# One redundant wait taken out of VectorE's program in a decode-block kernel

## The chip, the cores and the metric

The kernel runs on one core of one Trainium2 chip. The metric is the device time of one execution in microseconds; medians and ranges over several runs are given. VectorE is DVE in the profile, TensorE is PE (PEld for its weight loads), ScalarE is ACT, GpSimd is POOL, SyncE is SP. A letter q behind an engine's name means its sequencer.

## The reference, cut to what matters

One token (x, 640 wide) passes an attention block with a key and value cache and then a gated feed-forward block, each behind a layer norm:

```
h  = x + A(layernorm(x), k_cache, v_cache, wq, wo)   # 32 heads, 4096 cached positions, 128 wide
h2 = h + B(layernorm(h), w_gate, w_up, w_down)       # 640 -> 1728 -> 640
```

The caches and the weights are 84 MB, each byte used once. Only the first layer norm, that of x, has to do with the change.

## The kernel before: the parts concerned

The kernel records operations with their dependencies and emits waits for them. An operation whose function is `None` is a wait and nothing else.

```python
def _run(self, e, eng, ops, seen):
    for x in ops:
        ...
        for sem, c in self._need(eng, deps, seen).values():
            e.wait_ge(sem, c)
            seen[sem.name] = c
        if fn is None:
            continue
        inst = fn(e)
        if ev.used:
            inst.then_inc(ev.sem, 16 if ev.dma else 1)
```

GpSimd zeroes the tile `xlnB` first, then sets constants. TensorE spreads x over the partitions (`x_cols`), VectorE copies that out of PSUM, squares it, and so on to the normalised x, which is written into parts of `xlnB`:

```python
c_xz = GP(lambda e: e.memset(xlnB[:, :, :], 0.0))
c_one = GP(lambda e: e.memset(one_bf[:, :], 1.0))
...
xt = T(x_cols, d_x, c_one)
xc = V(lambda e: e.tensor_copy(xx[:, 0:5], ps_s[:, 0:5]), xt)

def layernorm(src, ev, out_fn, between=lambda: None):
    s2 = V(lambda e: e.tensor_mul(src[:, 5:10], src[:, 0:5], src[:, 0:5]), ev)      # "the square"
    m = T(lambda e: e.matmul(ps_s[:, 16:26], mean_f[:, :], src[:, 0:10], start=True, stop=True), s2, c_mean)
    ...                                                                             # 2 on VectorE, 2 on ScalarE
    return V(out_fn, l4)

xz = P.op("vector", None, c_xz)
xl = layernorm(xx, xc, lambda e: e.tensor_scalar(xlnB[...], xx[...], ln[:, 0:1], ln[:, 4:5], ALU.subtract, ALU.mult))
...
qd = T(q_proj, xl, d_wq)                       # the query projection, reads xlnB and wq
qa = VR(lambda e: e.tensor_copy(qb[...], ps_q), qd)
load_v(0, qd)                                  # first value load: into the place of wq
```

The softmax here doesn't subtract the row's maximum and nothing guards it: scores larger than these inputs give would overflow.

Of the kernel before, what the change touches and what calls it, by code (L numbers as in the profile page):

```python
# [180 lines left out]
def bass_sequential_preLN__gqa_block_cached__glu_gated_geglu__decode_kernel(nc, A_x, A_k_cache, A_v_cache, A_wq, A_wo, B_x, B_w_gate, B_w_up, B_w_down, out):  # L181
# [59 lines left out]
    P = Prog(nc)  # L241
# [31 lines left out]
    c_xz = GP(lambda e: e.memset(xlnB[:, :, :], 0.0))  # L273
# [56 lines left out]
    def layernorm(src, ev, out_fn, between=lambda: None):  # L330
        s2 = V(lambda e: e.tensor_mul(src[:, 5:10], src[:, 0:5], src[:, 0:5]), ev)
        m = T(lambda e: e.matmul(ps_s[:, 16:26], mean_f[:, :], src[:, 0:10], start=True, stop=True), s2, c_mean)
        l1 = V(lambda e: e.reduce_sum(ln[:, 0:2], ps_s[:, 16:26].rearrange("p (a c) -> p a c", a=2), axis=AX.X), m)
        l2 = V(lambda e: e.scalar_tensor_tensor(out=ln[:, 2:3], in0=ln[:, 0:1], scalar=ln[:, 0:1],
                                                in1=ln[:, 1:2], op0=ALU.mult, op1=ALU.subtract), l1)
        l3 = A(lambda e: e.activation(ln[:, 3:4], ln[:, 2:3], ACTF.Ln, bias=eps_t[:, 0:1], scale=-1.0), l2, c_eps)
        l4 = A(lambda e: e.activation(ln[:, 4:5], ln[:, 3:4], ACTF.Exp, bias=zero_t[:, 0:1], scale=-0.5), l3)
        between()
        return V(out_fn, l4)

    xz = P.op("vector", None, c_xz)
    xl = layernorm(xx, xc, lambda e: e.tensor_scalar(
        xlnB[:, :, :].rearrange("p c (a b) -> p c a b", a=4)[:, :, 0:4:3, :],
        xx[:, 0:5].unsqueeze(2).unsqueeze(3).to_broadcast([128, 5, 2, 16]), ln[:, 0:1], ln[:, 4:5],
# [257 lines left out]
```

## Time and profile before

| | before |
|---|---|
| time, median of 6 runs | 202.12 us (202.02 to 202.57) |
| span of the profiled run | 200.9 us |
| input queue's share of the DMA engines | 97.7% |
| VectorE busy | 103.6 us (52%) |
| wait records on VectorE's sequencer | 6 |
| copy of x to square of x, start to start | 0.28 us |

The lines behind the table stand in the prediction below. In the chain that ended last (the work followed back from the last instruction, each step to what released it), a row has a start, a length and what filled it; "issue" is time in which an engine waited for nothing that the profile shows. Rows of that chain near the end of the kernel before (VectorE's sequencer is DVEq), which the prediction did not look at, matter later:

```profile
196.33 0.03 issue
196.36 0.02 DVEq L114
196.38 0.04 issue
196.42 0.18 DVE hm L545
```

The second gate group ends on TensorE at 196.31 us (193.55 + 2.76 by the timeline), VectorE's sequencer serves a wait of 0.02 us, and 0.04 us later `hm` starts.

```profile
198.42 0.23 PEld L552 LDWEIGHTS psum<-k_all,hm 128*1 128x1 bf16 x12 [0.38 <-DMA k_all<-in_B_w_down_dram]
```

Here the down projection, started by `hm`, had to wait 0.38 us for a piece of its weights. So `hm` had a little time to spare in this execution, by this row up to 0.38 us as an estimate.

### The profile page before, as it was taken

What the parts mean: (1) busy time and instruction counts of PE and PEld (TensorE: products, weight loads), DVE (VectorE), ACT (ScalarE), POOL (GpSimd) and SP (SyncE); (2) the same over time, 40 slices, a digit from 0 to 9 for tenths busy, and PEclk for the clock granted to TensorE, in tenths of its full rate; (3) what the DMA queues carried; (4) which work ended last, traced back from release to release, by engine and by line L of the source; (5) the groups of instructions that cost most, each with busy time, mean ns of one, the idle gap of its engine ahead of it and who ended that gap; (6) DMA issues with size and microseconds to landing.
All of it is one profiled execution on the core that took longest, in us unless ns stands there. A gap on an engine that the chain in (4) does not pass through costs nothing.

```text
span 200.9 us, 2115 instructions
## 1 busy us (share of the span) xinstructions
PE 135.1 (67%) x1118; PEld 29.8 (15%) x742; DVE 103.6 (52%) x58; ACT 9.4 (5%) x27; POOL 7.4 (4%) x32
## 2 busy tenths in 40 slices
PE   0108001889897228997974588987899787787675
PEld 0103000000003100000022000000400000377573
DVE  0200001999942029799430599967798967020320
ACT  2100000000000100000001000000100000100100
POOL 6500000000000000000000000000000002000000
PEclk9999999999999855899999599999999999965555
DMA  9999999999999999999999999899999999999992
GB/s 351 424 478 418 418 418 418 418 431 496 483 447 418 418 431 418 418 418 418 431 418 418 483 483 444 346 424 424 418 516 418 418 418 401 416 436 417 427 404 98
DMA packets 2699, 84.31 MB, mean 420 GB/s; under 512 B 323, under 2 KB 518, under 8 KB 902
## 3 DMA queue, kind: packets, MB, share of 16 engines
q1 hardware_dynamic: 2690, 84.23, 97.7%
q8 instruction: 4, 0.07, 0.1%
q14 instruction: 1, 0.01, 0.0%
q10 hardware_dynamic: 4, 0.00, 0.0%
HBM read 84.23 MB, written 0.00 MB: 419 GB/s over the span
## 4 chain that ended last, share of the span: by engine, by line
DMA 65%; DVE 23%; PE 11%; issue 0%; ACT 0%; SPq 0%; DVEq 0%
DMA k_all<-in_A_k_cache_dram 42%; DVE prod L405 20%; DMA v_all<-in_A_v_cache_dram 13%; DMA v_all<-in_B_w_up_dram 9%; PE psum L167 4%; PE psum L389 4%; PE psum L531 1%; PE psum L552 1%; DVE sc L417 1%; DVE p_bd L424 1%; DVE sc L414 1%; DVE sc L415 1%; PE psum L371 0%; SPq L59 0%; ACT pt L418 0%
## 5 line engine op out<-in xcount | busy, mean ns | idle before, releaser
L405 DVE TENSOR_TENSOR prod<-k_all,qb 128x8192 bf16<-128x8192 bf16 x16 | 70.2, 4420 | 40.0 <-DMA k_all<-in_A_k_cache_dram 38.9
L167 PE MATMUL psum<-prod,id_b 128*128 128x512 bf16 x240 | 55.9, 387 | 0.0
L167 PE MATMUL psum<-none_b 128*128 128x512 bf16 x132 | 34.9, 419 | 0.0
L378 PE MATMUL psum<-none_b 128*128 128x512 bf16 x4 | 2.2, 549 | 26.1 <-DMA k_all<-in_A_k_cache_dram 26.1
L389 PE MATMUL psum<-v_all,p_bd 128*32 128x512 bf16 x256 | 14.5, 380 | 5.4 <-DVE p_bd L424 3.6
L417 DVE TENSOR_REDUCE sc<-psum 128x128 f32<-128x2048 f32 x6 | 13.7, 2286 | 5.2 <-PE psum L167 5.2
L371 PE MATMUL psum<-prod,id_b 128*128 128x512 bf16 x16 | 6.4, 400 | 9.5 <-DVE prod L405 6.7
L371 PEld LDWEIGHTS psum<-prod,id_b 128*128 128x128 bf16 x16 | 1.5, 96 | 75.5 <-DVE prod L405 47.9
L389 PEld LDWEIGHTS psum<-v_all,p_bd 128*32 128x32 bf16 x256 | 6.7, 97 | 37.5 <-DVE p_bd L424 31.6
L424 DVE TENSOR_TENSOR p_bd<-pt,own 128x1024 bf16<-128x1024 bf16 x8 | 9.8, 1221 | 2.2 <-ACT pt L418 2.2
L418 ACT ACTIVATE pt<-sc,zero_t 128x128 bf16<-128x128 f32 x8 | 3.2, 401 | 138.8 <-DVE sc L417 119.0
L354 PE MATMUL psum<-v_all,xlnB 128*32 128x512 bf16 x40 | 4.5, 630 | 6.7 <-DMA v_all<-in_A_wq_dram 6.7
L501 PE MATMUL psum<-aP,k_all 128*128 128x1 bf16 x160 | 6.7, 178 | 1.3 <-DMA k_all<-in_A_wo_dram 1.3
L460 POOL TENSOR_TENSOR RT<-RS,own 128x64 f32<-128x64 f32 x1 | 1.3, 1324 | 161.0 <-ACT pt L418 161.0
L501 PEld LDWEIGHTS psum<-aP,k_all 128*128 128x128 bf16 x160 | 6.6, 131 | 1.4 <-DMA k_all<-in_A_wo_dram 1.4
L395 PE MATMUL psum<-hs,po_sb 128*128 128x8 f32 x32 | 4.2, 258 | 3.2 <-ACT po_sb L458 3.2
L531 PE MATMUL psum<-hlnT,v_all 128*128 128x1 bf16 x150 | 5.5, 173 | 1.2 <-DMA v_all<-in_B_w_up_dram 1.2
L363 DVE CAST qb<-psum 128x512 bf16<-128x512 f32 x1 | 0.7, 690 | 9.7 <-PE psum L354 9.7
L531 PEld LDWEIGHTS psum<-hlnT,v_all 128*128 128x128 bf16 x150 | 5.4, 120 | 1.8 <-DMA v_all<-in_B_w_up_dram 1.3
L325 PE MATMUL psum<-one_bf,x_row 1*128 1x1 bf16 x5 | 0.4, 177 | 7.1 <-POOL own_g L308 7.1
L414 DVE TENSOR_REDUCE sc<-psum 128x64 f32<-128x1024 f32 x2 | 2.4, 1224 | 5.2 <-PE psum L167 5.2
L395 PEld LDWEIGHTS psum<-hs,po_sb 128*128 128x128 f32 x32 | 3.9, 191 | 5.1 <-issue 5.1
(75 smaller groups left out, 34.1 us busy)
## 6 DMA issues: line engine op xcount, KB each, us to landing
k_all<-in_A_k_cache_dram SPq DMA_DIRECT2D x2, 4096.0 KB, 20.6
v_all<-in_A_wq_dram SPq DMA_DIRECT2D x1, 5120.0 KB, 15.1
k_all<-in_A_wo_dram SPq DMA_DIRECT2D x2, 2560.0 KB, 29.2
v_all<-in_B_w_gate_dram SPq DMA_DIRECT2D x1, 2160.0 KB, 13.5
v_all<-in_B_w_up_dram SPq DMA_DIRECT2D x1, 2160.0 KB, 18.3
k_all<-in_B_w_down_dram SPq DMA_DIRECT2D x1, 800.0 KB, 21.0
k_all<-in_B_w_down_dram SPq DMA_DIRECT2D x1, 640.0 KB, 19.5
k_all<-in_B_w_down_dram SPq DMA_DIRECT2D x1, 480.0 KB, 21.7
```

The lines of the kernel that those rows point to most:

```text
L167: built = e.matmul(out, lhsT, rhs, start=start, stop=stop)
L354: i = e.matmul(ps_q[32 * t:32 * t + 32, :], xlnB[:, c, 32 * a:32 * a + 32], wq_j[:, c, t, a, :, :], start=(c == 0 and a == 0), stop=(c == ...
L371: mm = held if n or not first else lambda e, *a, **k: e.matmul(*a, **k)
L389: i = e.matmul(ps_o[a:a + 32, :], p_bd[:, s, 4 * b:4 * b + 4, :].rearrange("p g j -> p (g j)"), vt[:, 4 * b:4 * b + 4, :], start=(s == 0 a ...
L395: i = e.matmul(ps_a[:, bass.ds(at, 8)], po_sb[:, 128 * r:128 * r + 128], hs[:, r, :], start=(r == 0), stop=(r == 3))
L405: mults[j, s, i] = VM(lambda e: e.tensor_tensor(out=prod[:, i, :, :], in0=kt[:, 64 * c:64 * c + 64, :], in1=qb[:, j, :].unsqueeze(1).to_br ...
L414: V(lambda e: e.reduce_sum(sc[:, 64:128], g16(0, 1024), axis=AX.X), folds[j, s, 1], free)
L417: reds[j, s] = VR(lambda e: e.reduce_sum(sc[:, :], g16(0, 2048), axis=AX.X), folds[j, s, 1], free)
L418: exps[j, s] = AS(lambda e: e.activation(pt[:, :], sc[:, :], ACTF.Exp, bias=zero_t[:, 0:1], scale=INV_SQRT_DH, accum_out=RS[:, 2 * j + s:2 ...
L424: blocks[j, s] = VB(lambda e: e.tensor_tensor(out=p_bd[:, hf, :, :], in0=pt[:, :].unsqueeze(2).to_broadcast([128, 128, 8]), in1=own8[:, :] ...
L501: r = e.matmul(ps_p[:, c:c + 1], wo_sb[:, i, c::5], aP[:, i:i + 1], start=False, stop=(i == 31), skip_group_check=True)
L531: i = e.matmul(ps[:, m:m + 1], ws, hlnT[:, c:c + 1], start=(c == 0 and m == 0), stop=(c == 4), skip_group_check=True)
```

## The change

The tile is zeroed on GpSimd before `one_bf` is set: in the trace of the kernel before the two end at 1.64 and 1.66 us. TensorE's `x_cols` waits for `one_bf` (it starts at 7.09 us) and VectorE's copy waits for `x_cols` (7.48 us), so what stands behind the copy ran behind the zeroing too. By these times the wait is redundant; that the two always end in this order was not shown beyond the traces. The change takes the wait out to make VectorE's program one instruction shorter.

```diff
@@ -338,7 +338,6 @@
         between()
         return V(out_fn, l4)
 
-    xz = P.op("vector", None, c_xz)
     xl = layernorm(xx, xc, lambda e: e.tensor_scalar(
```

## The prediction

Marks in the text show passages that were cut afterwards: what it said about the chip without a trace or a run of this case that shows it, and one remark on the size of the first rival. What goes on with "it holds six such records" is about the trace of the kernel before and its records of waits (EventSemaphore). The sum came to 0.08 us saved off the path, 0.00 us on it, and so 202.04 us, put at 202.05. In the third rival the ground on which a stall was ruled out is cut, so that this rival stands there as not ruled out, with its figure of 203.0.

> **What bounds the kernel now.** I read the page's header and its DMA rows first, then the chain that ended last, then the order of work around the place that the diff touches, because the diff touches one place only.
>
> The header and the DMA rows say which engine could be the limit at all. From the page of the kernel before:
>
> ```profile
> span 200.9 us, 2115 instructions
> PE 135.1 (67%) x1118; PEld 29.8 (15%) x742; DVE 103.6 (52%) x58; ACT 9.4 (5%) x27; POOL 7.4 (4%) x32
> ...
> DMA  9999999999999999999999999899999999999992
> ...
> DMA packets 2699, 84.31 MB, mean 420 GB/s; under 512 B 323, under 2 KB 518, under 8 KB 902
> ...
> q1 hardware_dynamic: 2690, 84.23, 97.7%
> ```
>
> No compute engine is busy for more than 67% of the span, VectorE (DVE) for 52%. The DMA row shows 9 in 38 of 40 slices, one 8, and a 2 only in the last slice. The queue that carries the inputs keeps the 16 DMA engines busy for 97.7% of the span. So the kernel is a stream of 84.31 MB, and 84.31 MB at 420 GB/s is 200.7 us, the span to within 0.2 us.
>
> The chain that ended last, in order of time, shows what that means for the first stage (columns: start us, us, what):
>
> ```profile
> 0.00 0.41 SPq L59
> 0.41 0.05 issue
> 0.45 34.01 DMA k_all<-in_A_k_cache_dram
> 34.46 0.02 issue
> 34.49 13.10 DVE prod L405 x3
> ```
>
> The chain goes from SyncE's first issue straight to the first part of the key cache, which lands at 34.46 us. Nothing of the layer norm of x, where the changed line lies, is on it. The chain names VectorE for 23%, but at the later joints VectorE is only the way by which the next transfer is issued. I checked whether the queue runs dry while an issue waits on VectorE: the key load issued at 47.61 finds the first value load (issued at 19.78, 8.39 MB, started when the keys landed at 34.46) with some 7 us to go. That is an estimate: 8.39 MB at 420 GB/s is 20.0 us, so that load ends near 54.5. The same sum for the load issued at 88.52, behind a value load that starts at 74.19, leaves 5.7 us. Every later joint I worked out has about as much or more. So a shift of a tenth of a microsecond at VectorE doesn't reach the transfers.
>
> Now the place of the change, in the timeline of the kernel before (start us, us, engine, line, operation; in brackets the idle time before it and what ended it):
>
> ```profile
> 1.27 0.37 POOL L273 MEMSET xlnB<- 128x320 bf16 x1 [0.77 <-POOLq L587]
> ...
> 1.57 0.09 POOL L274 MEMSET one_bf<- 1x1 bf16 x1
> ...
> 7.48 0.17 DVE L328 COPY xx<-psum 128x5 f32<-128x5 f32 x1 [7.48 <-PE psum L325]
> 7.76 0.17 DVE L331 TENSOR_TENSOR xx<-xx 128x5 f32<-128x5 f32 x1
> ...
> 9.73 0.38 DVE L342 TENSOR_SCALAR xlnB<-xx,ln 128x160 bf16<-128x160 f32 x1 [0.69 <-ACT ln L337]
> ...
> 15.26 4.47 PE L354 MATMUL psum<-v_all,xlnB 128*32 128x512 bf16 x40 [6.68 <-DMA v_all<-in_A_wq_dram]
> ```
>
> The zeroed tile is ready at 1.64 us (1.27 + 0.37). The removed wait stands between the copy and the square of x at 7.76, six microseconds later: it never waits for anything. The normalised x is written by 10.11 us (9.73 + 0.38). Its reader, the query projection, starts at 15.26, and its idle time is ended by the DMA of wq, not by VectorE. So this stretch of VectorE has 15.26 - 10.11 = 5.15 us of slack.
>
> [...]it holds six such records on VectorE's sequencer, 21 ns each, and the first starts at 7.7 us, between the copy and the square. The compiled order of the two kernels shows the square waiting on two semaphores (VectorE's own and GpSimd's) before, and on VectorE's own alone after. So the instruction that goes is one of these six records.
>
> [...]GpSimd zeroes the tile first and sets one_bf second; TensorE's first matmuls wait for one_bf, and VectorE's copy waits for those matmuls. The trace agrees in that the two memsets end in that order (1.64 and 1.57 + 0.09 = 1.66), although their records overlap by 0.07 us.
>
> [...]
>
> [...]The instruction queue of this trace moved 4 packets and 0.07 MB, 0.1% of the DMA engines' time[...].
>
> **The change, part by part.**
>
> Removed: one wait instruction on VectorE. Its own record is 21 ns. What it costs is better read from a pair in the same trace: the copy and the square occur twice, once with the extra wait and once, in the second layer norm, without it.
>
> ```profile
> 186.67 0.17 DVE L507 COPY hT<-psum 128x5 f32<-128x5 f32 x1 [8.12 <-PE psum L501]
> 186.87 0.17 DVE L331 TENSOR_TENSOR hT<-hT 128x5 f32<-128x5 f32 x1
> ```
>
> With the wait the square starts 7.76 - 7.48 = 0.28 us after the copy started; without it, 186.87 - 186.67 = 0.20 us. So the wait costs about 0.08 us of VectorE's time, once. It is not in a loop.
>
> Also removed: the memset of the tile no longer raises a semaphore, because nobody is left that waits for it, and the counts that later waits on GpSimd's semaphore ask for are one lower. No instruction more or less comes of that on any other engine: the compiled lists of TensorE, ScalarE, GpSimd and SyncE have the same rows with the same waits in both kernels.
>
> Moved: the square, the mean matmul, the two small VectorE steps, the two activations and the write of the normalised x all come some 0.08 us earlier, so the write ends near 10.03 instead of 10.11. The projection still waits for wq at 15.26. The slack grows from 5.15 to 5.23 us, and the gain ends there. The copy that follows (out of PSUM, at 19.79) is released by the projection and keeps its time.
>
> Added: nothing. Sum: 0.08 us saved on a branch that is 5.15 us off the path; on the path 0.00 us. The time stays at 202.04 us, and what will be measured is the spread between runs: the three runs of before lie at 202.02, 202.04 and 202.51, a width of 0.49 us or 0.24%. I put the figure at 202.05, in the lower cluster.
>
> **The rivals.** First, the wait could be worth its 0.08 us in full, if this stretch of VectorE were on the path after all. Against it stands the DMA that ends the projection's idle time, 5 us later. The time would be 202.04 - 0.08 = 201.96, which the spread hides. [...]
>
> Second, another wait could take the place of the one removed: the square could now be held by its wait on the copy (VectorE's own semaphore). That wait is in the pair from the second layer norm as well, and there the gap from the end of the copy to the square is 0.03 us (186.87 - 186.84), so it would eat none of the 0.08. The time would be 202.04 again.
>
> Third, a shorter program could[...] stall VectorE somewhere. VectorE has 58 counted instructions and six of these waits plus a few of the start[...]. Were there a stall all the same, of 1 us say, it would have to fall outside the queue's margin of more than 5 us at the joints; only in the tail behind the last weights (from 193.5 us on) would it show, as 203.0.
>
> Fourth, TensorE's granted clock or the DMA rate could come out differently. The clock row of before falls to 5 tenths in a few slices, and in one of them the matmuls slow down and VectorE waits 1.1 us for them (at 84.07). [...]The joint it touched still had the 5.7 us of margin, so I give it no time in the middle stages. If the tail's clock or the DMA rate varied, it would vary in both kernels[...].
>
> **Range and chances.** The lower edge takes the best case of 0.08 us and 0.26 us of variation: 201.70. The upper edge takes the highest run of before and 0.09 us beyond: 202.60. To leave the band of 2% the time would have to move by 4.04 us, eight times the spread seen and fifty times the cost of the wait. I give 1% to each side for something that I do not see at all.
>
> **What would show it right or wrong.** In the changed kernel's profile: the first event-semaphore record of VectorE near 7.7 us is gone and five are left; the square starts 0.20 us after the copy in the first layer norm, as in the second; the write of the normalised x ends near 10.03; the projection still starts near 15.26 with its idle time ended by the DMA of wq, and that idle time is slightly longer; the chain still begins with the key load landing near 34.46; 84.31 MB at about 420 GB/s. The prediction is wrong if the projection's start or the landing of the first keys moves by more than the runs' spread, if the queue shows a slice in the middle below 8, or if the tail behind the last weights (193.5 to 200.9) changes its length by more than 0.5 us.

## More of the kernel before

The end of VectorE's work comes into the story later. It is the product `hm` behind the second gate group of matmuls (`up`), and the last copy out of PSUM:

```python
g9 = V(lambda e: e.tensor_mul(hm[:, :], gu[:, :], ps_u[:, 0:15]), g6, up)
...                                            # TensorE: the down projection reads hm
os = [V(lambda e: e.tensor_copy(out_row[0:33, 0:160], ps_d[0:33, 0:160]), dn[1]),
      A(lambda e: e.copy(out_row[0:33, 160:320], ps_d[64:97, 0:160]), dn[3])]
```

## The result, and the profile after

The changed kernel takes 202.22 us (median of 6 runs, 202.15 to 202.85), the kernel before 202.12. The ratio is 1.0004 with a 95% interval of 0.9988 to 1.0021: the same within 2%. Ratios here are the mean time of one kernel's fast runs over that of the other's fast runs of the same rounds, so not quite the ratio of the medians quoted.

| | before | after |
|---|---|---|
| time, median of 6 runs | 202.12 us | 202.22 us |
| lowest run | 202.02 us | 202.15 us |
| wait records on VectorE's sequencer | 6 | 5 |
| copy to square of x, start to start | 0.28 us | 0.20 us |
| query projection starts | 15.26 us | 15.44 us |
| first keys landed | 34.46 us | 34.63 us |
| wait row to `hm`: "issue" between them | 0.04 us | 0.46 us |

The page of the changed kernel, its header and DMA rows:

```profile
span 201.0 us, 2114 instructions
...
DMA packets 2699, 84.31 MB, mean 419 GB/s; under 512 B 323, under 2 KB 518, under 8 KB 902
...
q1 hardware_dynamic: 2690, 84.23, 97.6%
```

One instruction less, the same bytes at the same rate. The timeline of the changed kernel at the place of the change:

```profile
7.19 0.16 DVE L328 COPY xx<-psum 128x5 f32<-128x5 f32 x1 [7.19 <-PE psum L325]
7.39 0.17 DVE L331 TENSOR_TENSOR xx<-xx 128x5 f32<-128x5 f32 x1
...
9.36 0.38 DVE L341 TENSOR_SCALAR xlnB<-xx,ln 128x160 bf16<-128x160 f32 x1 [0.69 <-ACT ln L337]
...
15.44 4.47 PE L353 MATMUL psum<-v_all,xlnB 128*32 128x512 bf16 x40 [7.23 <-DMA v_all<-in_A_wq_dram]
```

The square starts 7.39 - 7.19 = 0.20 us after the copy, so 0.08 us came out. The rest of the shift of the normalised x (it is ready at 9.74, not at 10.11) is not the change: the copy itself starts 0.29 us earlier, because x landed earlier in this execution (TensorE's first weight load, released by the DMA of x, starts at 6.80 us, in the kernel before at 7.09). The projection waits for wq in both kernels; here it starts 0.18 us later.

The chain near the end is where the kernels differ in a way that nobody had asked for:

```profile
196.24 0.03 issue
196.26 0.02 DVEq L114
196.28 0.46 issue
196.74 0.18 DVE hm L544
```

Same wait, same product, but 0.46 us of "issue" between them where the kernel before has 0.04. The whole stretch from the start of the second gate group to the last copy out of PSUM on VectorE is 199.29 - 193.48 = 5.81 us in the changed kernel and 199.18 - 193.55 = 5.63 before. So of 0.42 us more, some 0.2 us reached the end; the kernel before spends part of that time waiting for the last weights anyway, as its row above shows. Over all traces in which nothing else holds up that copy, the stretch is 5.43 to 5.68 us in the nine without the gap and 5.76 to 5.84 us in the four with it.

### The profile page after: what moved, and what is told of

It is laid out like the page before. It is cut to its first block, busy times and chain, and to the rows that moved or that the text cites. A ratio compares the mean times of both kernels' runs of the same rounds, so it can differ in the third digit from the quotient of the medians.

```text
span 201.0 us, 2114 instructions
## 1 busy us (share of the span) xinstructions
PE 135.3 (67%) x1118; PEld 29.8 (15%) x742; DVE 103.5 (52%) x58; ACT 9.3 (5%) x27; POOL 7.3 (4%) x32
## 2 busy tenths in 40 slices
DMA packets 2699, 84.31 MB, mean 419 GB/s; under 512 B 323, under 2 KB 518, under 8 KB 902
## 4 chain that ended last, share of the span: by engine, by line
DMA 65%; DVE 23%; PE 11%; issue 1%; ACT 0%; SPq 0%; DVEq 0%
DMA k_all<-in_A_k_cache_dram 42%; DVE prod L404 20%; DMA v_all<-in_A_v_cache_dram 13%; DMA v_all<-in_B_w_up_dram 9%; PE psum L167 4%; PE psum L388 4%; PE psum L530 1%; DVE sc L416 1%; PE psum L551 1%; DVE p_bd L423 1%; DVE sc L413 1%; DVE sc L414 1%; PE psum L370 0%; SPq L59 0%; ACT pt L417 0%
## 5 line engine op out<-in xcount | busy, mean ns | idle before, releaser
(75 smaller groups left out, 33.6 us busy)
```

## The experiments

Twelve runs were made. They came in four batches, and each batch has runs of the kernel before beside it on the same chip. Theory: the wait lay on a branch with time to spare, so nothing reaches the end. First rival: the shorter program itself costs something. Unless told otherwise an edit is against the changed kernel, and results agree with the reference.

**The kernel before against itself, and the changed kernel again.** No edit.

> The kernel before against itself, to measure how far two identical kernels differ in five rounds. Both theories: ratio 1.000, interval within 0.002 either side, single runs between 202.0 and 202.9 us. A ratio of 1.0004 (the figure of the changed kernel) or more would show that that figure is noise.

> The changed kernel once more. Theory (the wait lies on a branch with 5 us to spare): ratio 0.999 to 1.001, and the square again starts 0.20 us after the copy. Rival (the shorter program itself costs something, which is why the first measurement was 0.04% above): ratio 1.0004 or more again, with an interval that leaves out 1.

The kernel before against itself gave a ratio of 1.0032 with an interval of 1.0001 to 1.0064. Identical kernels were told apart by 0.3%, because single executions run up to 203.84 us. So a mean over such rounds can't resolve less than about 0.3%, and the interval that excludes 1 is here a false alarm. The changed kernel gave 1.0029 (0.9996 to 1.0063), no more than that.

The lower edges tell more, though they were looked at after the fact. On this one chip, 8 of 11 runs of the kernel before lie between 201.92 and 202.07, and 3 of 6 runs of its copy at or below 202.14. No run of the changed kernel is below 202.18 (and none of the first six below 202.15). Over all batches, 26 of the 42 runs of the kernel before lie below 202.15, and none of the 12 of the changed kernel. A shift of some 0.2 us upwards is what the stretch at the end had suggested. My theory did not have it; the third rival of the prediction had a stall there, but with 203.0 us. In the repeated trace the "issue" ahead of `hm` is 0.46 us again, and in the trace of the copy of the kernel before `hm` starts 0.11 us after the gate group's end as in the first.

**The two waits of the square swapped, in the kernel before.**

```diff
+    xz = P.op("vector", None, xc)
     xz = P.op("vector", None, c_xz)
```

> The kernel before, with the two waits ahead of the square in the other order: the compiled list has the extra wait instruction on GpSimd's semaphore (raised at 1.6 us) and the square itself carries the wait on the copy. In the kernel before it is the other way round. Theory A (the 0.08 us came from the wait on the copy standing in an instruction of its own): six wait records on VectorE as before, but the first is served early, and the square starts 0.20 us after the copy as if it were not there. Theory B (any extra wait instruction costs its 0.08 us): 0.28 us. Time in both: ratio 0.999 to 1.001.

In these lists an instruction that computes holds one wait; the other goes into an instruction of its own in front. The compiled lists show which:

```
before:   EventSemaphore waits VectorE >= 1 (the copy);  square waits GpSimd >= 1 (the zeroing)
swapped:  EventSemaphore waits GpSimd >= 1 (the zeroing); square waits VectorE >= 1 (the copy)
after:    square waits VectorE >= 1 (the copy)
```

The timeline of the swapped kernel, and the records of waits on VectorE's sequencer:

```profile
7.42 0.17 DVE L328 COPY xx<-psum 128x5 f32<-128x5 f32 x1 [7.42 <-PE psum L325]
7.62 0.17 DVE L331 TENSOR_TENSOR xx<-xx 128x5 f32<-128x5 f32 x1
```

```profile
L114 DVEq EVENT_SEMAPHORE  x6: 21/21/21, 7.4 to 196.2; - x6
```

All six wait records are there, the first at 7.4 us (in the kernel before it is at 7.7, behind the copy), and the gap is 0.20 us: theory A. What cost 0.08 us was not the redundant wait but that it pushed the needed one, on the copy, into an instruction of its own, so that after the copy's end first a wait and then the square had to be served. Ahead of the copy's end the same wait instruction cost nothing here: the gap is 0.20 us with it as without it. The time, ratio 1.0006 (0.9987 to 1.0025), says nothing more.

**An empty instruction where the wait stood.**

```diff
+    idle("vector", 1)
     xl = layernorm(xx, xc, ...
```

> The changed kernel with one empty instruction on VectorE where the wait stood: the program has its old length and not its old wait. Theory: the square starts 0.20 us after the copy, since nothing waits; ratio 0.999 to 1.001. Rival (the length of the program matters): the kernel before's gap of 0.28 us.

The program has the old length and the gap is 8.94 - 8.74 = 0.20 us, so length does not make the gap. Time: 202.04 us beside 202.11, ratio 0.9989 (0.9963 to 1.0016), three of four runs below 202.09. And the "issue" ahead of `hm` is 0.04 us, as before the change (chain):

```profile
196.22 0.04 issue
196.26 0.18 DVE hm L545
```

One empty instruction, nearly 190 us earlier, takes the 0.46 us away. That is where the second theory below came from.

**Forty waits instead of one, off the path and on it.** The waits are on a semaphore that the instruction in front has to raise (the copy of x, or TensorE's end), so all but the first are satisfied when read. Eighty were asked for; the compiler put them in pairs, which makes forty instructions (2154 in the pages, 2114 in that of the changed kernel).

```diff
+    def many(n, ev):
+        ev.used = True
+        def fn(e):
+            for _ in range(n):
+                i = e.wait_ge(ev.sem, ev.count)
+            return i
+        return P.op("vector", fn)
+    many(80, xc)            # first kernel: ahead of the first layer norm
+    many(80, dn[1])         # second kernel: ahead of the last copy out of PSUM
```

> The changed kernel with forty satisfied wait instructions between the copy and the square, on the copy's own semaphore, where one was removed. Theory (5 us to spare): the square starts 0.8 to 3.2 us later than 0.20 us after the copy (forty times 0.02 to 0.08 us), the projection still starts near 15.3 us, the time stays: ratio 0.998 to 1.002. Rival (waits on VectorE here do reach the end): 0.8 to 3.2 us more, ratio 1.004 to 1.016.

> The changed kernel with the same forty wait instructions ahead of the last copy out of PSUM, which is on the path. Theory: the time grows by exactly what the forty cost in the other kernel, 0.8 to 3.2 us (203.0 to 205.4). Rival ([...]they cost nothing anywhere): 202.2.

Off the path (timeline):

```profile
7.32 0.16 DVE L328 COPY xx<-psum 128x5 f32<-128x5 f32 x1 [7.32 <-PE psum L325]
11.44 0.17 DVE L331 TENSOR_TENSOR xx<-xx 128x5 f32<-128x5 f32 x1 [3.96 <-issue]
```

The square comes 4.12 us after the copy, 3.92 us later than without: 0.098 us for each of the forty, more than I had expected (I had 3.2 us as the most). The time is 202.06 us, ratio 0.9986 (0.9937 to 1.0034): nothing of it arrives. On the path (timeline, the two last copies, which start within 0.04 us of each other in both traces of the result):

```profile
199.72 0.29 ACT L575 CAST out_row<-psum 33x160 bf16<-33x160 f32 x1 [6.13 <-PE psum L167]
203.60 0.32 DVE L574 CAST out_row<-psum 33x160 bf16<-33x160 f32 x1 [6.29 <-issue]
```

VectorE's copy is 3.88 us behind its twin, and the time is 206.36 us beside 202.10, ratio 1.0219 (1.015 to 1.0288), more than the 205.4 that I had as the most. Whether it is over 2% is unclear, that it is slower is not. The same forty instructions cost about four microseconds at the end of the program and nothing at its start. That the waits are cheap is thus not why the change moved nothing.

**How much the branch has to spare.** Products of 0.82 us ahead of the first square, ten in the first kernel and twenty-nine in the second:

```diff
+        if src is xx:
+            for _ in range(10):            # 29 in the second kernel
+                ev = V(lambda e: e.tensor_tensor(out=hX[...], in0=id_f[...], in1=ones_f[...], op=ALU.mult), ev, c_idf)
         s2 = V(lambda e: e.tensor_mul(src[:, 5:10], src[:, 0:5], src[:, 0:5]), ev)
```

> The changed kernel with ten VectorE products of 0.82 us ahead of the first square: about 8.5 us, more than the 5.15 us of slack that the prediction gave to this stretch. Theory 1 (the slack that counts runs on to the moment at which the key load ends and the first value load must have been issued, near 34.5, some 14 us later): the projection starts near 18.3 instead of 15.3, the first value load is issued near 22.8 instead of 19.9, the time stays: ratio 0.998 to 1.002. Theory 2 (the slack ends with the landing of wq): 8.5 - 5.15 = 3.4 us more, ratio 1.017.

> The same with twenty-nine products, about 24.7 us, past both slacks. Both theories: slower. Theory 1: the first value load is issued near 39.1, 4.6 us after the key load has landed, so the stream stands still for 4.6 us and the start of a transfer, and the time grows by 5 to 7 us (207 to 209). Theory 2: 24.7 - 5.15 = 19.6 us more (221.8).

With ten the normalised x is late for the projection (timeline):

```profile
18.45 4.04 PE L357 MATMUL psum<-v_all,xlnB 128*32 128x512 bf16 x36 [1.58 <-DVE xlnB L345]
```

Now VectorE ends its wait, and the first value load is issued at 22.97 us. The time is 202.11 us beside 202.10, ratio 0.9991 (0.9944 to 1.0038): theory 1. The 5.15 us of the prediction were true but not the whole: what the branch must meet is the moment at which the stream of loads would run dry.

With twenty-nine the time is 210.26 us, ratio 1.0403 (1.0345 to 1.0461), so 8 us more, somewhat above theory 1's 5 to 7 and far from theory 2's 19.6. The first value load is issued at 38.65 us, and the stream stands still (page, GB/s in 40 slices of 5.2 us):

```profile
GB/s 371 386 454 403 492 504 13 202 403 403 416 545 441 405 403 416 403 454 466 466 416 403 416 403 429 504 366 410 454 448 416 492 479 314 425 429 417 429 406 113
```

The seventh and eighth slice move 13 and 202 GB/s: of 10.4 us about 7.7 are lost (1 - 215/840, with 420 as full rate). I had let the standstill begin at 34.5 us, where the keys land in the other kernels; the row shows that most of the stream had run out by 31.2 us, the start of the seventh slice, which fits a loss larger than expected. So the delay is felt once it reaches the loads.

**Fewer bytes.**

```diff
-        landed["V", j] = P.dma("sync", v_all[:, 0:2 * HALF], src, *after, chan="V")
+        n = 2 * HALF if j != 1 else 2 * HALF * 7 // 8
+        landed["V", j] = P.dma("sync", v_all[:, 0:n], src[:, 0:n], *after, chan="V")
```

> The changed kernel with the second value load cut to seven eighths (1.05 MB less of 84.31; the result is wrong on purpose in the rows of those heads). Theory (the stream of transfers is the limit from one end to the other): 1.05 MB at 420 GB/s is 2.5 us less, 199.7 us, ratio 0.988. Rival (the joints, where VectorE releases the next load, set the pace): nothing gained, 202.2.

200.33 us beside 202.11, which is 1.8 us less by the medians; by the ratio of the means, 0.9893 (0.9863 to 0.9924), it is 2.2 us. Both are under the 2.5 expected. The result still passed as correct, which I had not expected and did not look into. So here 1.05 MB less in the stream counted, and a VectorE instruction less beside it did not.

**Where the 0.4 us ahead of `hm` comes from.** After thirteen traces (two with the result, eleven from the runs above, the next one and the long program told last) there was a pattern. The programs whose VectorE instructions up to `hm` are just as many as in the changed kernel, in the same order (the changed kernel twice, the forty waits behind `hm`, the fewer bytes), have 0.46 us of "issue" ahead of `hm`. Those with 1, 10, 29, 40 or 280 more, all forms of the kernel before among them, have 0.04. Theory F, an assumption at this point: there are places in VectorE's program, called boundaries here, ahead of which VectorE loses some tenths of a microsecond, and `hm` came to stand right behind one. In the changed kernel the wait ahead of `hm` starts at 196.26 us, with the gate group just ended (at 196.23), so time lost behind that wait is seen in full. One instruction more, and the wait itself stands behind the boundary: the loss falls where VectorE waits for TensorE anyway (in the kernel before it is idle for 2.42 us ahead of `hm`).

Two runs speak to it. One had been made with the first four, for the sake of the swapped waits alone: the two waits of `hm` change places.

```diff
-    g9 = V(lambda e: e.tensor_mul(hm[:, :], gu[:, :], ps_u[:, 0:15]), g6, up)
+    g9 = V(lambda e: e.tensor_mul(hm[:, :], gu[:, :], ps_u[:, 0:15]), up, g6)
```

> The changed kernel, with the two waits ahead of the last product of the gate stage (hm) swapped, so that the instruction itself carries the wait on TensorE and the separate one the wait on VectorE's own product, long satisfied. This one is on the chain that ended last. Theory A of the swapped wait: the gap from the end of TensorE's second gate group to hm falls by 0.05 to 0.08 us in the trace. Theory B: unchanged. Time: at most 0.08 us less, 0.04%, which five rounds will hardly tell: ratio 0.999 to 1.001.

The program is as long as the changed kernel's, but the separate wait is now the one long satisfied (it is served at 194.4 us), and `hm` itself waits for TensorE. Chain:

```profile
197.47 0.02 issue
197.49 0.18 DVE hm L544
```

The gap from the gate group's end (194.69 + 2.76 = 197.45) to `hm` is 0.04 us, against 0.11 before and 0.51 after the change. The 0.07 below the kernel before is the swapped wait again; the rest fits theory F, since the separate wait is served at 194.37 us and a loss behind it falls into the 3.08 us in which TensorE still works. The times don't show it: 202.24 us, ratio 1.0012 (0.9982 to 1.0041), although three of its six runs lie below 202.15 and its lowest, 201.82, is the lowest of all that load the full bytes. The profiled execution was one of its longer ones (203.09), with late weights.

The second run shifts everything by 256 empty instructions in a stretch where VectorE waits for keys (14.81 us in its trace):

```diff
+    idle("vector", 256)
     load_v(0, qd)
```

> The changed kernel with 256 empty instructions on VectorE after the copy of the queries out of PSUM, in a stretch where VectorE has nothing to do until the first keys land near 34.5 us. It asks two things. First, the gap from the end of TensorE's second gate group to the product hm: so far it was 0.51 to 0.52 us in the four programs whose VectorE stream up to hm is that of the changed kernel, and 0.11 us in the eight with 1, 10, 29, 40 or 280 instructions more. Theory F (hm is the first instruction behind a boundary[...], so one instruction less put it there): a shift by 256 brings the 0.52 us back. Rival (any longer program has 0.11): 0.11 us. Second, the 1.9 us that the program with 280 empty instructions at the start lost. [...]If its late first copy had a part in it, this one, which leaves the layer norm on time, takes 202.0 to 202.4.

Two passages of this text are cut: what theory F said the boundary is and at what distance it recurs, which nothing had shown then, and a sentence on the second question that put the cost down to the further packets of a queue (told below). The latter's figure was 203.5 to 204.2 us.

Chain of that kernel:

```profile
198.37 0.40 issue
198.78 0.18 DVE hm L545
```

The gap is back (0.47 us from the gate group's end, where 0.52 was expected). Had any longer program 0.11 us there, it would not be. So it is shown that the 0.4 us depend on where in VectorE's program `hm` stands, that one instruction more removes them and 256 more restore them.

The same trace also shows breaks among its empty instructions. These are their records (operation NOP), asked for from 19.9 to 22.8, from 22.8 to 29.5 and from 29.5 to 33.6 us; each row has their number, the ns that one takes (18) and when the first and the last start:

```profile
L317 DVEq NOP  x55: 18/18/18, 20.0 to 22.6; - x55
L317 DVEq NOP  x128: 18/18/18, 23.0 to 29.0; - x128
L317 DVEq NOP  x73: 18/18/18, 30.0 to 33.4; - x73
```

They start 0.047 us apart, but for two breaks: 0.47 us after the first 55 and 1.04 us after 128 more. From the second break to `hm` it is 73 empty instructions and 55 others (50 that compute and 5 waits), so 128 again. The program with 280 empty instructions, told below, has breaks of 0.47 and 0.55 us among them, also 128 apart. In both traces the first break stands ahead of the 64th instruction that is recorded for VectorE, waits and empty ones counted. In the changed kernel the 64th is `hm`; in the kernel before it is the wait ahead of `hm`. So in these traces a break recurs every 128 recorded instructions, takes 0.47 to 1.04 us among empty instructions and leaves 0.40 to 0.46 us of "issue" ahead of `hm` where no waiting hides it, and the change moved `hm` behind the first. These places are the boundaries of theory F.

What happens at a boundary was not shown. The page lists a second queue of the kind "instruction", q14, and a packet of 8192 bytes on it moves with VectorE's program: it starts at 193.45 us in the kernel before, ahead of `hm`; at 197.59 after the change, behind `hm`; at 156.7 with ten products more. And 256 instructions more go with two packets more, one for each 128. The packets come after the breaks, by 3.7 to 5.3 us among the empty instructions, and by 0.7 to 1.4 us after `hm` starts in the five traces with the gap. With `hm`'s waits swapped it is 3.2 us after the wait ahead of `hm` was served (197.54 against 194.37), which fits. So `hm` can't have been waiting for that packet, and what fills the 0.4 us at a boundary is open.

**A long program.** That run also had to explain an earlier surprise: 280 empty instructions at the start of VectorE's program.

```diff
+    idle("vector", 280)
     xc = V(lambda e: e.tensor_copy(xx[:, 0:5], ps_s[:, 0:5]), xt)
```

> The changed kernel with 280 empty instructions at the start of VectorE's program[...]. Rival[...]: a stall on VectorE somewhere behind, time over 202.2 by 0.5 us or more. Theory: they run while VectorE would sit idle until 7 us anyway, or push the first copy back by a few us within its slack; time stays, ratio 0.998 to 1.002[...].

The rival is that a longer program costs time.

It took 204.04 us beside 202.11, ratio 1.0086 (1.006 to 1.0112): the rival's figure, 1.9 us more. The first copy moved to 15.38 us, a delay of 8.2 us, but the ten products above delay as much and cost nothing. From its page and its chain:

```profile
q14 instruction: 3, 0.02, 0.0%
```

```profile
0.46 35.11 DMA k_all<-in_A_k_cache_dram
```

Three packets on that queue where the other kernels have one (the other queue of its kind, q8, of which I had expected a fifth packet, stays at four), two of them at 9.4 and 14.8 us among the first loads, and the keys land at 35.57 us; in the eleven traces without a longer program or the twenty-nine products they land between 34.25 and 34.84. The run with 256 leaves the layer norm on time and has three such packets too, two of them at 28.3 and 34.0 us. There the keys land at 35.49 us, and the time is 203.40 us beside 202.08, ratio 1.0056 (1.0036 to 1.0076). That is just under the 203.5 to 204.2 expected if the two packets more cost it, and well over the 202.0 to 202.4 expected if the late copy had a part. So the late copy is not needed for the loss, and a longer program with more packets among the loads goes with later keys. Whether the packets or the empty instructions themselves do it, these runs can't tell. Why the keys land some 1 us later (a packet of q14 takes 0.31 us in the two traces of the result), and why the two kernels differ by 0.6 us, stays open.

## Why the prediction was right, and where it was not

- **The bound.** Right. The stream sets the time: 1.05 MB less took 1.8 to 2.2 us off, while 3.9 us more of VectorE's time ahead of the projection added nothing (202.06 us beside 202.10).
- **The cost of the wait, 0.08 us.** Right in size (0.28 to 0.20 us in the trace), wrong in kind. It belongs to a needed wait that stands in an instruction of its own; with the waits swapped the redundant one costs nothing (0.20 us again).
- **The slack, 5.15 us.** Right as a lower bound. The ten products, 8.6 us, went by without a trace, as the loads still had work queued (the first value load was issued at 22.97 us, the keys landed at 34.46); the twenty-nine did not (38.65 us). The margin of some 7 us at the first joint was too high: it lets the first value load start at 34.46 us, while the row of the twenty-nine products shows the loads ahead of it all but done by 31.2. That leaves 3 to 4 us as an estimate, still far over 0.08.
- **The sum, "on the path 0.00 us".** This term was missized. The removed wait gave nothing, but the shift of the program put 0.42 us ahead of `hm`, on the chain that ends last, and about 0.2 us of it reached the end. That the time stayed in the stated range is no merit of this term: the range had been set from the spread of runs, which is wider.
- **The third rival, a stall from a shorter program.** This is the step that failed. I had ruled the stall out by an assumption that no trace of this case shows, and which is cut. The traces show a break ahead of the 64th recorded instruction of VectorE and, in the two long programs, one every 128 further; the change moved `hm` from the 65th place to the 64th. The four packets that I read as the instruction queue are those of q8, which stay four in every run; the one that moves with VectorE's program is on q14. The size that I gave such a stall (1 us, 203.0) was too large, and its place, the tail behind the last weights, was right.
- **The second rival.** The wait on the copy did take the place of the removed one, and cost nothing (0.20 us from copy to square, as in the second layer norm), as said.
- **What would be seen.** Five wait records, 0.20 us, the projection released by wq, 84.31 MB at 419 GB/s: as said. The normalised x ended at 9.74 and not near 10.03, because x landed 0.29 us earlier. The tail from the landing of the last gate weights grew by less than the 0.5 us that I had named as a limit, so the test I set was too coarse to find the stall.

Versions that beat both kernels by more than the spread of runs were not found. The best guess from the traces is the changed kernel with `hm`'s waits swapped.

## What to carry to other kernels

Where an instruction has two waits, try the order in which the one that comes last is held by the instruction itself, and the other, in an instruction of its own, is served while there is nothing else to do: here that took the gap ahead of the square from 0.28 to 0.20 us, and the one from the gate group to `hm` to 0.04 us, where it had been 0.11 before the change and 0.51 after it. A change of a single instruction can move another, far behind it: here one removed ahead of the first square put 0.42 us ahead of `hm`, nearly 190 us later. So look at the gaps of the last chain in both traces before calling a difference noise. And before trusting a small ratio, run the kernel against itself.
